# TensorE chooses among code versions by each expert's token count, in a kernel of local attention and a top-2 mixture of experts

## The chip, the cores and the metric

The kernel runs on one core of a Trainium2 chip. Besides TensorE (matmuls), VectorE (DVE), ScalarE (ACT) and GpSimd (POOL), SyncE (SP) issues DMAs, and 16 DMA engines move data between HBM and the on-chip memories. Each engine runs its own instruction stream, in order, and waits for others on semaphores. Matmul results go to PSUM, which has eight banks of 512 f32 columns by 128 partitions.

The metric is the device time of one execution in microseconds. Before the change three runs gave 741.88, 744.48 and 735.51 us, median 741.88.

## What is computed

Attention over four sequences of 768 tokens with eight heads (a local window of 16 and block summaries) gives 3072 tokens of 512 values. These go through a mixture of eight experts. Each token picks its two best experts by a noisy gate, and each expert applies two products with a ReLU between them:

```python
    N, D, E, F = (3072, 512, 8, 1024)
    ...
    logits = x @ w_gate
    noise_scale = np.log1p(np.exp(x @ w_noise))
    noisy_logits = logits + noise_scale * noise
    top2 = np.argpartition(-noisy_logits, 2, axis=1)[:, :2]
    ...
    for e in range(E):
        for k in range(2):
            mask = top2[:, k] == e
            if not mask.any():
                continue
            h = np.maximum(x[mask] @ w1[e], 0.0)
            out[mask] += top2_w[mask, k, None] * (h @ w2[e])
```

The mean count is 3072 x 2 / 8 = 768 tokens for an expert. With the reference's default inputs the counts are 728, 793, 748, 801, 765, 779, 756 and 774.

## The kernel before

The attention stage goes over 24 tiles of 128 tokens and takes the first 176 us or so. The gate runs beside it, in six batches; it gives each token a slot in each of its two experts' lists. An expert has `CAP = 816` slots. What does not fit goes to an overflow block at the end (L1023 to L1033), which is jumped over when `nover`, a count computed on VectorE in `count_over` (L552 to L564), is zero; all five engines load that count into a register (L1023) and branch on it (L1024). With the default inputs no expert overflows.

Then the experts follow one after another (L953 to L966). For expert e:

- `x_gather` (L625) fetches the tokens' rows from HBM by index, on GpSimd's queue, 128 slots at a time; `x_trans` (L636) transposes them into `xte` by a DMA on SP's queue.
- `mm1(e, half, f)` (L642 to L656) computes 128 of the 1024 hidden values, `f` from 0 to 7, for one half of the slots: columns 0 to 384 in half 0, 384 to 816 in half 1, so 384 or 432 columns. Weights and tokens are split into two f16 parts, so one `f` is 12 matmuls (three pairings of parts times four chunks of 128 input values), all on line 650, into one PSUM bank. ScalarE then writes the ReLU (`hth`, L654) and VectorE the remainder (`htl`, L655), over all columns of the half.
- `mm2(e, c, pv)` (L680 to L706) computes the second product for 128 slots, `c` from 0 to 5: 24 matmuls of 512 columns (L696). The last piece, `c == LAST == 6`, has only 48 slots. It is done as 48 matmuls of 256 columns (L692), two at a time in two halves of the output partitions. VectorE scales the result by the gate weight and adds the earlier sum (L703), and GpSimd scatters it to the output (L86).
- `prev_gather` fetches the earlier sums, and `next_loads` spreads the next expert's weight loads, splits and gathers over the steps of this one.

The first expert differs in order: its half 0 is computed while the last gate batches are still decoded, three pieces of its second product come ahead of its half 1 (L930 to L942).

The order of instructions on each engine is the order in which the code issues them, written out by hand. All choices are made at build time but the overflow block: every expert is computed for all 816 slots, whether a token stands in them or not; empty slots carry an index out of bounds, which the scatter drops.

PSUM is shared: two buffers `pt` for the second product, and a pool of four banks `h` for the first product and the last gate pieces (L872), opened when the attention's own buffers are given back (L871).

## Time and profile before

| what | value |
|---|---|
| median of 3 runs | 741.88 us |
| profiled execution | 741.86 us |
| its span, first to last instruction | 740.1 us |
| mean granted TensorE clock | 0.963 |
| attention and gate, about | 0 to 176 us |
| first two experts, with weight loads | 176 to 325 us |
| experts 2 to 7, each | 67.05 us |
| a hidden tile of half 0 / half 1 on TensorE | 1.95 / 2.19 us |
| the piece of 48 slots on TensorE | 2.74 us |

The page gives for each engine the busy time and its share of the span; then the span in 40 slices; the DMA queues; the chain of work that ended last, followed back from the last instruction to what released it at each step; and groups of instructions by line. "q8 instruction" is a DMA queue that brings code, not data. Names such as PEldq, DVEq or SPq mean an engine's sequencer: register loads, branches and semaphore instructions, which are not counted as busy time. PEld is the weight load that goes with each matmul and overlaps the matmul before it. A matmul's listed duration is longer than the distance from one start to the next, since matmuls are pipelined; the cost of one in a stream is that distance.

### The profile page before, as it was taken

To read this page: it belongs to the slowest core of one execution; us is meant where nothing else is said; L and a number is where in the kernel's file an instruction comes from. 1 tells how busy PE (TensorE), PEld (TensorE's weight loads), DVE (VectorE), ACT (ScalarE), POOL (GpSimd) and SP (SyncE) were. 2 spreads that over 40 slices of the span, in tenths; PEclk is the share of its full clock that TensorE was granted. 3 is DMA by queue.
4 is the path that set the end of the run, shared out by engine and by line. 5 is a ranking of instruction groups with operands and counts; after the bars stand their busy time and mean duration, and the time that the engine had idled before them with its cause. 6 is when DMAs were issued, how large, how long until landed. Compare 5 with 4: busy or idle time off the path is not lost.

```text
span 740.1 us, 13612 instructions
## 1 busy us (share of the span) xinstructions
PE 694.0 (94%) x5330; PEld 409.2 (55%) x5330; DVE 323.2 (44%) x686; ACT 234.8 (32%) x523; POOL 283.1 (38%) x464
## 2 busy tenths in 40 slices
PE   7979897887989999999999999999999999999992
PEld 6667686765535555455446545554654555455441
DVE  6647868685934344234414431541353143412210
ACT  3568766771404044024203310430242033102100
POOL 2566556443040550553234243414432342340141
PEclk9999988985999999999999999999999999999997
DMA  9998987273269698569826941993497289511020
GB/s 284 283 281 249 278 230 215 92 186 122 88 156 364 207 276 195 151 179 222 235 84 162 198 169 65 192 224 131 112 214 180 86 169 163 159 47 38 23 80 33
DMA packets 105418, 126.21 MB, mean 171 GB/s; under 512 B 63701, under 2 KB 68445, under 8 KB 105344
## 3 DMA queue, kind: packets, MB, share of 16 engines
q1 hardware_dynamic: 93200, 88.96, 48.0%
q0 software_dynamic: 12144, 36.28, 18.1%
q8 instruction: 44, 0.72, 0.5%
q14 instruction: 30, 0.25, 0.1%
HBM read 88.14 MB, written 26.36 MB: 155 GB/s over the span
## 4 chain that ended last, share of the span: by engine, by line
PE 73%; DMA 11%; DVE 9%; SPq 1%; ACT 1%; POOL 1%; issue 1%; POOLq 0%; DVEq 0%
PE h L650 32%; PE pt L696 29%; PE pt L692 3%; DMA vw<-in_vt_dram 2%; PE o L337 2%; DMA htl<-in_vb_dram 2%; PE s L304 2%; DMA stg<-in_vb_dram 2%; PE pt L324 1%; PE o L378 1%; DMA stg<-in_w_dram 1%; DMA xd<-xr 1%; DMA xg<-xd,tb 1%; DVE w1l L596 1%; DVE w2l L596 1%
## 5 line engine op out<-in xcount | busy, mean ns | idle before, releaser
L650 PE MATMUL h<-xte,w1h 128*128 128x432 f16 (+1 forms) x1024 | 201.9, 338 | 3.6 <-DVE htl L655 2.9
L654 ACT ACTIVATE hth<-h 128x432 f16<-128x432 f32 (+1 forms) x128 | 63.7, 507 | 287.9 <-PE h L650 284.7
L86 POOL DMA_INDIRECT out_dram<-y,tb x48 | 53.4, 1113 | 244.7 <-DVE y L703 214.0
L650 PEld LDWEIGHTS <-w1h 128*128 128x128 f16 x1024 | 99.9, 98 | 81.1 <-issue 7.2
L696 PEld LDWEIGHTS <-hth 128*128 128x128 f16 x768 | 75.1, 98 | 91.8 <-issue 2.3
L655 DVE SCALAR_TENSOR_TENSOR htl<-h,hth 128x432 f16<-128x432 f32 (+1 forms) x128 | 73.2, 580 | 96.2 <-ACT hth L654 94.5
L650 PE MATMUL h<-xte,w1l 128*128 128x432 f16 (+1 forms) x512 | 109.9, 338 | 0.0
L703 DVE SCALAR_TENSOR_TENSOR y<-pt,tb,prev 128x512 f32<-128x512 f32 x42 | 31.5, 750 | 149.2 <-PE pt L696 149.2
L86 POOL DMA_INDIRECT xg<-xd,tb x56 | 58.9, 1052 | 95.9 <-DMA xte<-xg 59.7
L696 PE MATMUL pt<-w2l,hth 128*128 128x512 f16 x384 | 91.0, 379 | 1.5 <-DVE w2l L596 1.5
L696 PE MATMUL pt<-w2h,htl 128*128 128x512 f16 x384 | 90.7, 379 | 0.0
L696 PE MATMUL pt<-w2h,hth 128*128 128x512 f16 x384 | 90.7, 379 | 0.0
L650 PEld LDWEIGHTS <-w1l 128*128 128x128 f16 x512 | 50.3, 98 | 38.8 <-issue 0.9
L587 ACT ACTIVATE w2h<-stg 128x1024 f16<-128x1024 f32 x32 | 33.8, 1055 | 92.4 <-DMA stg<-in_w_dram 92.4
L696 PEld LDWEIGHTS <-htl 128*128 128x128 f16 x384 | 37.6, 98 | 45.3
L596 DVE SCALAR_TENSOR_TENSOR w2l<-stg,w2h 128x1024 f16<-128x1024 f32 x32 | 39.1, 1222 | 52.5 <-ACT w2h L587 51.8
L86 POOL DMA_INDIRECT prev<-out_dram,tb x42 | 46.9, 1116 | 10.9 <-issue 10.9
L318 ACT ACTIVATE p<-s,nm 128x118 f32<-128x118 f32 x192 | 50.5, 375 | 0.8
L358 POOL TENSOR_TENSOR xr<-x,xr 128x512 f16<-128x512 f32 x24 | 30.3, 1261 | 50.6 <-ACT xr L355 43.3
L596 DVE SCALAR_TENSOR_TENSOR w1l<-stg,w1h 128x1024 f16<-128x1024 f32 x32 | 41.7, 1302 | 15.3 <-ACT w1h L587 12.3
L337 PE MATMUL o<-vw,pts 118*64 118x65 f32 x768 | 34.9, 247 | 5.7 <-DMA vw<-in_vt_dram 5.6
L337 PEld LDWEIGHTS o<-vw,pts 118*64 118x64 f32 x768 | 30.3, 158 | 11.8 <-DMA vw<-in_vt_dram 8.3
(164 smaller groups left out, 641.9 us busy)
## 6 DMA issues: line engine op xcount, KB each, us to landing
stg<-in_w_dram SPq DMA_DIRECT2D x64, 512.0 KB
vw<-in_vt_dram SPq DMA_DIRECT2D x48, 195.0 KB
q<-in_qt_dram SPq DMA_DIRECT2D x24, 256.0 KB
xd<-xr SPq DMA_DIRECT2D x24, 256.0 KB
kb<-in_kt_dram SPq DMA_DIRECT2D x6, 768.0 KB
out_dram<-prev SPq DMA_DIRECT2D x6, 768.0 KB
htl<-in_vb_dram SPq DMA_DIRECT2D x6, 390.0 KB
hth<-in_vb_dram SPq DMA_DIRECT2D x5, 390.0 KB
```

What stands on the lines that cost most here:

```text
L86: return nc.gpsimd.indirect_dma_start(**kw)
L318: nc.scalar.activation(PE_[t][:, a, hp, :], SC[t][:, a, hp, :], AF.Exp, bias=NM[t][:, 1, a, hp:hp + 1], scale=0.125)
L337: nc.tensor.matmul(o[64 * blk:64 * blk + 64, h // 4, c:c + D + 1], PT[t][:NK, h % 2, h // 2, 64 * blk:64 * blk + 64], VX[t][blk][:NK, h, : ...
L358: nc.gpsimd.tensor_tensor(XR[t][:, DM:], X[t], XR[t][:, 0:DM], op=OP.subtract)
L587: nc.scalar.activation(WT[e][n + "h"][:, i % 4, :], SG[e, i], AF.Copy, scale=sc)
L596: nc.vector.scalar_tensor_tensor(lo, SG[e, i], sc, hi, op0=OP.mult, op1=OP.subtract)
L650: nc.tensor.matmul(ph[:, :n], w[wn][:, c, f * P:(f + 1) * P], x[:, xo + c, c0:c1], start=(k == 0), stop=(k == 11))
L654: nc.scalar.activation(hh[:, f, c0:c1], ph[:, :n], AF.Relu)
L655: nc.vector.scalar_tensor_tensor(hl[:, f, c0:c1], ph[:, :n], 0.0, hh[:, f, c0:c1], op0=OP.max, op1=OP.subtract)
L692: nc.tensor.matmul(py[64 * i:64 * i + 64, :HD], hx[:, f, c * P:c * P + 64], wv[:, f, HD * i:HD * i + HD], start=(k == 0), stop=(k == 23), ...
L696: nc.tensor.matmul(py, hx[:, f, c * P:c * P + P], wv[:, f, :], start=(k == 0), stop=(k == 23))
L703: nc.vector.scalar_tensor_tensor(y, py[:, :d], gw, pv[:, :d], op0=OP.mult, op1=OP.add)
```

## The change

The first product's second half exists in four versions, ending at slot 744, 768, 792 or 816, with 360, 384, 408 or 432 columns. VectorE works out in `count_over`, by comparing each expert's count with 744, 768 and 792, which version an expert needs, and by comparing with 768 whether its last 48 slots are used at all; both numbers go to `arms`. TensorE loads the two into registers ahead of an expert's half 1 (`pick`). It then chooses by the first for each `f` of half 1, so eight times an expert, among four copies of the 12 matmuls, and by the second once an expert, whether the 48 matmuls of the last piece run. TensorE alone takes part in the choice; the other engines run the same instructions as before, over all 816 slots.

As the four banks and the two `pt` buffers are now written inside the versions, they are tiles set up once and taken in turn. VectorE clears columns 384 to 432 of the four banks once, since a narrow version leaves the last columns unwritten.

```diff
+    WIDTHS = range(744, CAP + 1, 24)
...
+        k = len(WIDTHS) - 1
+        ge = work.tile([P, E, k], F32, name="ge", bufs=1)
+        nc.vector.tensor_tensor(ge, cf[:, :, None].to_broadcast([P, E, k]),
+                                edges[:, None, :].to_broadcast([P, E, k]), op=OP.is_gt)
+        ga = work.tile([P, E, 2], F32, name="ga", bufs=1)
+        nc.vector.tensor_reduce(ga[:, :, 0], ge, axis=AX.X, op=OP.add)
+        nc.vector.tensor_scalar(ga[:, :, 1], cf, float(LAST * P), None, op0=OP.is_gt)
+        nc.vector.tensor_copy(arms, ga)
...
+    def pick(e):
+        _, v = nc.values_load_multi_w_load_instructions(
+            arms[0:1, e, :], engines=[mybir.EngineType.PE], min_val=0, max_val=len(WIDTHS) - 1,
+            skip_runtime_bounds_check_because="sums of comparisons, at most one for each edge")
+        ARM[e] = [{mybir.EngineType.PE: x} for x in v]
...
+    def mm1(e, half, f):
+        c0, c1 = (0, H0) if half == 0 else (H0, CAP)
+        ph = bank()[:, 0]
+        if half == 0:
+            mm1_mul(e, f, ph, c0, c1)
+        else:
+            for i in tc.Switch(ARM[e][0], len(WIDTHS)):
+                mm1_mul(e, f, ph, c0, WIDTHS[i])
+        mm1_out(f, ph, c0, c1)
...
-        py = psum.tile([P, 512], F32, name="pt", bufs=2)
+        py = back()
...
+        if last:
+            for i in tc.Switch(ARM[e][1], 2):
+                if i:
+                    mul()
+        else:
+            mul()
...
-    banks.append(ctx.enter_context(tc.tile_pool(name="banks", bufs=4, space=PSUM, reuse_waits="tile")))
+    bpool = ctx.enter_context(tc.tile_pool(name="banks", bufs=1, space=PSUM, reuse_waits="tile"))
+    for i in range(4):
+        x = bpool.tile([P, 1, 512], F32, name=f"h{i}")
+        nc.vector.memset(x[:, 0, H0:CAP - H0], 0.0)
+        banks.append(x)
...
+    pick(0)
     for f in range(FC):
         mm1(0, 1, f)
...
         for half in range(2):
+            if half:
+                pick(e)
             for f in range(FC):
                 mm1(e, half, f)
```

`mm1_mul` holds the 12 matmuls and `mm1_out` the ReLU and the remainder, as they stood in `mm1` before; `mul` holds the second product's matmuls. `bank` and `back` return the fixed tiles in turn.

## The prediction

> **What bounds the kernel now.** I read the page first (engine shares, clock, chain), then the chain of waits in order of time, then a table by stretch, then the single rows of TensorE.

> ```profile
> span 740.1 us, 13612 instructions
> PE 694.0 (94%) x5330; PEld 409.2 (55%) x5330; DVE 323.2 (44%) x686; ACT 234.8 (32%) x523; POOL 283.1 (38%) x464
> PE h L650 32%; PE pt L696 29%; PE pt L692 3%; DMA vw<-in_vt_dram 2%; PE o L337 2%; DMA htl<-in_vb_dram 2%; PE s L304 2%; DMA stg<-in_vb_dram 2%; PE pt L324 1%; PE o L378 1%; DMA stg<-in_w_dram 1%; DMA xd<-xr 1%; DMA xg<-xd,tb 1%; DVE w1l L596 1%; DVE w2l L596 1%
> ```

> Two thirds of the chain that ends last are the two expert products on TensorE. In order of time that chain is

> ```profile
> 178.13 3.87 PE h L650 x12
> 458.69 33.23 PE h L650 x192
> 491.91 31.08 PE pt L696 x144
> 522.99 2.74 PE pt L692 x48
> 724.19 2.76 PE pt L692 x48
> ```

> and by stretch (columns: length, busy time and count by engine, granted clock, DMA share, GB/s)

> ```profile
> 175.70:290.80 115.10, 109.01 (x623) 59.77 (x622) 57.49 (x141) 32.47 (x52) 31.14 (x55) 0.97 0.76 216
> 340.20:357.82 17.62, 17.62 (x98) 9.43 (x97) 9.07 (x12) 8.40 (x13) 7.49 (x12) 1.00 1.12 287
> 458.69:525.73 67.04, 67.04 (x385) 35.35 (x386) 23.30 (x31) 15.73 (x24) 24.54 (x42) 1.00 0.73 160
> ```

> An expert from the second on is 33.23 + 31.08 + 2.74 = 67.05 us of TensorE without a gap, at full clock; VectorE has 23.3 us of work in it, ScalarE 15.7, GpSimd 24.5, the DMA engines 0.73 of the time. So in this stage every microsecond put on or taken off TensorE moves the end by as much, and nothing else is near to becoming the bound.

> **What is taken away.** The second half of the first product is eight times 12 matmuls of 432 columns (L650), the first half of 384:

> ```profile
> 461.88 1.46 PE L650 MATMUL h<-xte,w1h 128*128 128x384 f16 x8
> 463.83 1.46 PE L650 MATMUL h<-xte,w1h 128*128 128x384 f16 x8
> 475.69 1.62 PE L650 MATMUL h<-xte,w1h 128*128 128x432 f16 x8
> 477.88 1.62 PE L650 MATMUL h<-xte,w1h 128*128 128x432 f16 x8
> ```

> From start to start 12 matmuls take 1.95 us at 384 and 2.19 us at 432 columns: 162.5 and 182.5 ns each, 0.417 ns a column. With the reference's default inputs I count 728, 793, 748, 801, 765, 779, 756 and 774 tokens for the eight experts. The versions end at 744, 768, 792 and 816 slots, so the experts save 72, 0, 48, 0, 48, 24, 48 and 24 columns, 264 in all: 264 x 96 matmuls x 0.417 ns = 10.6 us. The last 48 slots stay empty where the count is at most 768, in four experts: 4 x 2.74 = 11.0 us. Together 21.5 us, 2.9%, if choosing cost nothing.

> **What is added.** 64 choices among four versions (eight for each expert, one for each f) and 8 choices whether the last piece runs: 72 choices, so they may cost 21.5 / 72 = 0.30 us each before the gain is gone. Each choice is register arithmetic and a jump to the version on TensorE's own instruction stream, and a second jump from the version's end to the common code, past the versions that were not taken. The profile of before has one runtime condition, the overflow block at the end (L1023, L1024), which every engine jumps over:

> ```profile
> L1023 SPq FUSED_REGOPS  x1: 178/178/178, 632.2 to 632.2; - x1
> L1023 PEldq TENSOR_LOAD <-nover x1: 490/490/490, 725.6 to 725.6; - x1
> L1024 SPq EVENT_SEMAPHORE  x9: 2/17/17, 637.8 to 638.5; - x9
> L1024 POOLq EVENT_SEMAPHORE  x6: 17/30/43, 731.1 to 731.6; - x6
> L1024 ACTq EVENT_SEMAPHORE  x2: 17/17/17, 696.2 to 696.3; - x2
> L1024 PEldq EVENT_SEMAPHORE  x2: 51/51/51, 730.4 to 730.6; - x2
> L1024 DVEq EVENT_SEMAPHORE  x2: 21/21/21, 730.6 to 730.7; - x2
> L1024 SPq COMPARE_BRANCH  x1: 53/53/53, 632.6 to 632.6; - x1
> L1024 ACTq COMPARE_BRANCH  x1: 50/50/50, 693.7 to 693.7; - x1
> L1024 PEldq COMPARE_BRANCH  x1: 4162/4162/4162, 726.2 to 726.2; - x1
> L1024 DVEq COMPARE_BRANCH  x1: 72/72/72, 727.6 to 727.6; - x1
> L1024 POOLq COMPARE_BRANCH  x1: 62/62/62, 728.1 to 728.1; - x1
> ...
> q8 instruction: 44, 0.72, 0.5%
> ```

> The reader is to see that the branch itself lasts 50 to 72 ns on four engines, but the next instruction starts 5.2 us (SP), 2.5 (ACT), 2.9 (DVE) and 3.0 us (POOL) after it, and on TensorE the branch is recorded with the whole delay, 4.16 us. A jump over much code cost 2.5 to 5.2 us wherever it happened. The new jumps pass over less code (a version is 12 weight loads and 12 matmuls; the overflow block has 8 experts x 120 matmuls and as many weight loads), so whether they pay the same is the question on which all hangs. No row shows a short jump. I take 4.2 us, TensorE's own row; the ends are 0.05 us (the bare branches) and 5.2 us (SP's).

> [...]

> **How far TensorE's queue covers it.** The sequencer runs ahead of the array:

> ```profile
> L650 PEldq EVENT_SEMAPHORE  x22: 51/51/51, 177.9 to 672.6; - x22
> 659.89 33.23 PE h L650 x192
> ```

> The last wait that L650's sequencer handles, at 672.6, stands ahead of the second half, which starts on the array at 659.89 + 96 x 0.1625 = 675.5: a lead of 2.9 us, some 18 matmuls. Likewise the load of nover starts at 725.6 while the array works until 724.19 + 2.76 = 726.95. So a jump does not stop the array at once; the first 2.9 us of each half are covered. But a lead is refilled only if the sequencer needs less than the array for each f, and the array needs 1.8 to 2.2 us.

> **The sum.** One choice costs the sequencer S = 0.2 (register arithmetic, as SP's row) + 4.2 (jump in) + 4.2 (jump out) = 8.6 us; issuing the 12 pairs takes 12 x 2.74 / 48 = 0.7 us, which I let lie beside the fetch for the jump out. An f's matmuls run within that, even at half clock (the row 178.13: 12 matmuls in 3.87 us). So for an expert:
> - second half: two register loads 2 x 0.49 = 1.0, plus 8 x 8.6 = 68.8, less the lead 2.9, in place of 8 x 2.19 = 17.5: +49.4 us. The narrower matmuls then save nothing, since the array waits.
> - last piece: the lead in the second product is 18 x 31.08 / 144 = 3.9 us, against 4.4 for getting in: +0.5; then 4.2 out in place of 2.74, whether skipped or run: +1.5. Together +2.0.
> - the array works 2 of 8.6 us in that half and will drop to half clock for part of it, as in the row at 178.13; the second product then starts slow: estimate +2 (0 to 4).

> That is 53.4 us an expert, 8 x 53.4 = 427 us. In 175.70 to 290.80 the array idles 115.1 - 109.0 = 6.1 us on loads of the first two experts' weights; a later TensorE no longer waits there: -4.

> The small edits: four DVE instructions in count_over before the last copy,

> ```profile
> 199.73 0.33 DVE L559 TENSOR_TENSOR x<-cf,steps 128x168 f32<-128x168 f32 x1
> 200.65 0.17 DVE L564 CAST nover<-nf 128x9 int32<-128x9 f32 x1
> PE pt L696 <- DVE w2l L596: 1.5, 2, 1.0
> ```

> of 0.17 to 0.33 us, 0.8 us ahead of the split of w2 that TensorE waits for next: +0.8 (0 if the later work absorbs it). The four banks are now cleared by VectorE, once, 128x48 each, near 0.17 us by the small rows:

> ```profile
> 175.72 1.89 PE L378 MATMUL h<-wg,xt 128*128 128x16 f32 x8
> 177.04 0.32 DVE L522 TENSOR_TENSOR acc<-acc,o 128x168 f32<-128x168 f32 x1
> ```

> They stand behind L522 on VectorE, so the gate matmuls into the first bank can start at 177.36 + 0.34, not 175.72: +2.0, 0 if the waits after it absorb this. Fixed banks in turn, where the pool gave four before, and the two fixed tiles of the second product change no wait: the same four and two buffers with the same readers. One more iota on GpSimd lies at the start, where it has nothing due. No DMA is added or moved on SP's or GpSimd's queue; their gathers and scatters wait on TensorE's pace and stretch with it. ScalarE and VectorE still empty all 432 columns.

> Sum: 741.86 (profiled execution, span 740.1; the median of the runs is 741.88, the same) + 427 - 4 + 3 = 1168 us.

> **The rivals.**
> 1. The jump out costs little, because its target is asked for on entering the version or follows it at once. The bounds of S: jumps of 2.5 us (ACT's row) and a free way out give 0.2 + 2.5 + 0.7 = 3.4, +7.8 us for a half, about -1.4 for the last piece: 742 + 8 x 6.4 = 793; with 4.2 us in, S = 5.1 and about 742 + 8 x 22 = 918. For it: two jumps are not known to be equal. Against: 0.7 us of issue cannot cover a fetch of 4.2.
> 2. Faster, the other side: the versions lie so near that the jumps hit loaded code. Then S = 0.2 + 0.05 + 0.7 + 0.05 = 1.0 us, under the array's 1.8 to 2.2 us, the lead stays, and 742 - 21.5 + 3 = 723 us. This decides from S below about 1.9. For it: before, the instruction queue's 44 packets, 16 KB each, never show as idle time of TensorE, so straight code is fetched in time. Against: versions and jumps make the stream four times as long for the same work, and every jump row here is slow.
> 3. Jumps partly hit: S of 2.2 to 2.4, 0.2 us over the array for each f, about cancels the 11 us that the skipped pieces save, and the time is within 2%: some 740.
> That the kernel would not do what it says has no room of its own: were the counts higher, it would pay the same jumps.

> **How the numbers follow.** Forecast 0.76; rival 1 0.13; rival 2 0.07; rival 3 0.04. Slower by over 2% is forecast and rival 1: 0.89; within 2% (about what can be told from no change here): 0.04; faster: 0.07. Upper bound: SP's 5.2 us for both jumps and no overlap, S = 11.3, +71 for a half, +4 last piece, +4 clock: 742 + 8 x 79 = 1374. The likeliest one's own range is 918 (both jumps 2.5: S = 5.2, +22 an expert) to 1374. The range takes in the upper half of rival 1 and goes from 830 to 1400; left out are rivals 2 and 3 and the rest of rival 1.

> **What would show it.** Right: second halves of about 60 to 70 us for each expert with the 12 matmuls of an f together and gaps of some 6 us between, jumps of microseconds at the new lines of TensorE's sequencer, a granted clock of 0.5 there, more packets in the instruction queue than its 44 (one or two more for each choice), first halves unchanged at 15.6 us. Wrong in size: the first jump long and the second not. Wrong altogether: second halves of 15 to 17.5 us without gaps. Wrong in the cover: a gap already at the first f of the first half.

## The result, and the profile after

The changed kernel takes 1279.73 us (median of 4 runs, 1276.32 to 1281.57) against 743.18 us for the kernel before in the same series. The ratio is 1.7245, with a 95% interval of 1.711 to 1.7379. The profiled execution has a span of 1276.7 us, 536.6 more than before.

The page of the changed kernel, engine shares, granted clock by slice and the queue that brings code:

```profile
span 1276.7 us, 13978 instructions
PE 805.0 (63%) x5138; PEld 428.5 (34%) x5138; DVE 326.8 (26%) x694; ACT 234.5 (18%) x523; POOL 282.7 (22%) x465
...
PEclk9898969558866985689667966798569866797679
...
q8 instruction: 288, 4.72, 2.2%
```

TensorE runs 192 matmuls fewer and is busy 63% of a span that has grown by 73%; the other engines do the work they did before. From the eighth slice on, in which the choices begin, the clock drops to a half or two thirds again and again. The code queue has 288 packets instead of 44.

Who waited for whom on TensorE (total, times, longest):

```profile
PE h L675 <- issue: 386.2, 64, 15.9
PE h L675 <- DMA stg<-in_w_dram: 26.3, 4, 8.5
PE o L385 <- DVE lg L393: 8.4, 4, 4.0
```

L675 is the line of the first product's matmuls now. There are 64 waits, one for each choice of a version, 6.0 us in the mean, and they are put down to "issue": no other engine is late, TensorE's own instruction stream is. The sequencer's instructions around the choices, which the trace gives under L1126 (the line on which the program is closed), L685 and L740:

```profile
L1126 PEldq MOVE  x144: 29/29/34, 219.5 to 1258.1; - x144
L1126 PEldq COMPARE_BRANCH  x144: 299/4667/11380, 219.8 to 1264.0; - x144
L1126 ACTq COMPARE_BRANCH  x72: 32/33/33, 205.0 to 1229.9; - x72
L1126 DVEq COMPARE_BRANCH  x72: 41/41/53, 217.1 to 1256.9; - x72
L1126 PEldq FUSED_REGOPS  x72: 32/32/39, 219.7 to 1258.2; - x72
L1126 POOLq COMPARE_BRANCH  x72: 32/33/46, 222.2 to 1257.7; - x72
L1126 SPq COMPARE_BRANCH  x72: 20/33/113, 224.0 to 1032.3; - x72
...
L685 PEldq BRANCH_PREFETCH_HINT  x64: 31/40/50, 220.2 to 1225.9; - x64
...
L740 PEldq EVENT_SEMAPHORE  x4: 51/51/51, 315.4 to 1132.4; - x4
```

(The three numbers are the shortest, the middle and the longest duration in ns.) TensorE executes 144 branches, two for each of 72 choices. The middle one lasts 4.67 us, the longest 11.4. The register work beside them, moves and one fused operation, is some 30 ns each. TensorE is not alone in the choice, as I had described it: the four other engines pass each choice by a branch of their own, 20 to 113 ns.

What one choice looks like on the array, from the last expert's half, when the DMA engines are nearly idle:

```profile
1165.46 1.53 PE L675 MATMUL h<-xte,w1h 128*128 128x408 f16 x4 [7.59 <-issue]
1166.79 1.56 PE L675 MATMUL h<-xte,w1l 128*128 128x408 f16 x4
1168.15 1.56 PE L675 MATMUL h<-xte,w1h 128*128 128x408 f16 x4
1175.30 1.54 PE L675 MATMUL h<-xte,w1h 128*128 128x408 f16 x4 [5.59 <-issue]
```

The 12 matmuls of one f come together, at half clock (some 340 ns apart; at full clock 172 would do, between the 162.5 ns at 384 columns and the 182.5 at 432), and then the array is empty for 5.6 us. From one choice to the next it is 9.84 us. And by stretch, the same columns as before:

```profile
464.30:500.00 35.70, 8.17 (x25) 3.25 (x24) 4.13 (x5) 3.09 (x5) 5.74 (x10) 0.56 0.88 147
500.00:558.60 58.60, 21.85 (x72) 9.54 (x72) 7.17 (x9) 6.50 (x10) 0.00 (x0) 0.63 0.10 24
594.01:609.60 15.59, 15.59 (x86) 8.94 (x87) 5.62 (x8) 4.83 (x8) 8.90 (x17) 0.89 0.98 245
609.60:685.36 75.76, 36.04 (x109) 13.87 (x108) 11.40 (x14) 9.41 (x14) 2.10 (x4) 0.65 0.27 64
1136.26:1151.86 15.60, 15.60 (x86) 8.98 (x87) 3.35 (x6) 2.95 (x7) 3.33 (x6) 0.89 0.19 52
1151.86:1230.82 78.96, 31.38 (x108) 13.00 (x106) 5.69 (x10) 5.21 (x10) 0.00 (x0) 0.65 0.04 7
1230.82:1262.50 31.68, 31.25 (x144) 14.02 (x144) 4.43 (x7) 0.00 (x0) 10.05 (x18) 1.00 0.21 69
```

The first half of an expert still takes 15.6 us where the piece ahead of it was run. After a skipped piece it takes 17.3, as its first two f take 5.6 us instead of 3.9, at half clock for a part: the rows at 594.01 and 1136.26 have 86 of its 96 matmuls at a clock of 0.89, and its last 1.7 us lie in the rows behind them. The second half takes 94.3 us for one expert (the first two rows), 74.1 for the next and 77.3 for the last, where 17.5 stood before. The second product (the last row) is as before. In the first row the array got 25 matmuls in 35.7 us, while the DMA engines were busy 0.88 of the time.

### The profile page after: what moved, and what is told of

Its sections match the earlier page's. It is cut to its first block, busy times and chain, and to the rows that moved or that the text cites. A ratio compares the mean times of both kernels' runs of the same rounds, so it can differ in the third digit from the quotient of the medians.

```text
span 1276.7 us, 13978 instructions
## 1 busy us (share of the span) xinstructions
PE 805.0 (63%) x5138; PEld 428.5 (34%) x5138; DVE 326.8 (26%) x694; ACT 234.5 (18%) x523; POOL 282.7 (22%) x465
## 3 DMA queue, kind: packets, MB, share of 16 engines
q8 instruction: 288, 4.72, 2.2%
## 5 line engine op out<-in xcount | busy, mean ns | idle before, releaser
L675 PE MATMUL h<-xte,w1h 128*128 128x384 f16 (+3 forms) x1024 | 281.6, 420 | 421.4 <-issue 386.2
L675 PEld LDWEIGHTS <-w1h 128*128 128x128 f16 x1024 | 115.3, 119 | 561.2 <-issue 500.7
L86 POOL DMA_INDIRECT out_dram<-y,tb x48 | 57.0, 1187 | 793.2 <-DVE y L750 704.8
L692 ACT ACTIVATE hth<-h 128x432 f16<-128x432 f32 (+1 forms) x128 | 65.1, 509 | 889.3 <-PE h L675 856.3
L675 PE MATMUL h<-xte,w1l 128*128 128x384 f16 (+3 forms) x512 | 151.9, 436 | 0.0
L736 PE MATMUL pt<-w2h,hth 128*128 128x512 f16 x384 | 93.6, 388 | 6.2 <-ACT hth L692 6.2
L675 PEld LDWEIGHTS <-w1l 128*128 128x128 f16 x512 | 63.9, 125 | 64.2 <-issue 44.4
L86 POOL DMA_INDIRECT prev<-out_dram,tb x42 | 43.2, 1028 | 10.8 <-issue 10.8
L616 DVE SCALAR_TENSOR_TENSOR w1l<-stg,w1h 128x1024 f16<-128x1024 f32 x32 | 41.8, 1306 | 10.8 <-ACT w1h L607 9.7
L344 PE MATMUL o<-vw,pts 118*64 118x65 f32 x768 | 35.1, 249 | 5.4 <-DMA vw<-in_vt_dram 5.3
L344 PEld LDWEIGHTS o<-vw,pts 118*64 118x64 f32 x768 | 30.5, 160 | 11.3 <-DMA vw<-in_vt_dram 7.8
```

The lines of the kernel that those rows point to most:

```text
L86: return nc.gpsimd.indirect_dma_start(**kw)
L344: nc.tensor.matmul(o[64 * blk:64 * blk + 64, h // 4, c:c + D + 1], PT[t][:NK, h % 2, h // 2, 64 * blk:64 * blk + 64], VX[t][blk][:NK, h, : ...
L616: nc.vector.scalar_tensor_tensor(lo, SG[e, i], sc, hi, op0=OP.mult, op1=OP.subtract)
L675: nc.tensor.matmul(ph[:, :c1 - c0], w[wn][:, c, f * P:(f + 1) * P], x[:, xo + c, c0:c1], start=(k == 0), stop=(k == 11))
L692: nc.scalar.activation(hh[:, f, c0:c1], ph[:, :n], AF.Relu)
L736: nc.tensor.matmul(py, hx[:, f, c * P:c * P + P], wv[:, f, :], start=(k == 0), stop=(k == 23))
```

## The experiments

Ratios are against the kernel before, run in the same series.

**The same choices by conditions in line.** The same register, the same four versions, but no table:

```diff
-            for i in tc.Switch(ARM[e][0], len(WIDTHS)):
-                mm1_mul(e, f, ph, c0, WIDTHS[i])
+            v = ARM[e][0][mybir.EngineType.PE]
+            with tc.If(v < 2) as a:
+                with tc.If(v < 1) as b:
+                    mm1_mul(e, f, ph, c0, WIDTHS[0])
+                with b.Else():
+                    mm1_mul(e, f, ph, c0, WIDTHS[1])
+            with a.Else():
...
-            for i in tc.Switch(ARM[e][1], 2):
-                if i:
-                    mul()
+            with tc.If(ARM[e][1][mybir.EngineType.PE] > 0):
+                mul()
```

> The same choices with the same registers and the same versions, but made by nested two-way conditions whose code stands in line (a jump passes over 24 to 78 instructions) instead of a jump into a table; the last piece is one condition that jumps over 96 instructions. Code theory (the time goes into fetching code that a jump lands in, because each version of the table starts in code that is not loaded): short jumps land in loaded code, the sequencer stays ahead, both savings are kept but for what a jump now and then over the edge of the loaded code costs: 720 to 745 us, 728 the likeliest. Choice theory (any decision on TensorE's sequencer costs some 5 us, because the branch has to wait for the register or for the queue to run empty): 2 or 3 branches for each f, as slow as the table or slower: above 1200 us.

Measured: 749.66 us, ratio 1.014 (1.007 to 1.0211). The branches of this kernel on TensorE, by the line of the condition, and its code queue:

```profile
L686 PEldq COMPARE_BRANCH  x64: 73/147/3694, 220.5 to 695.0; - x64
...
L687 PEldq COMPARE_BRANCH  x64: 65/214/4764, 220.7 to 632.6; - x64
...
L692 PEldq COMPARE_BRANCH  x48: 70/176/298, 280.0 to 696.7; - x48
...
q8 instruction: 64, 1.05, 0.6%
```

More branches than in the table kernel, taken on the same values, and the middle one lasts 0.15 to 0.21 us instead of 4.67. The choice theory falls: neither reading the register nor deciding is slow. Of the 537 us all but 9 are gone, though the same versions stand in the program; their code came in 64 packets instead of 288.

The times of the code packets in both traces show what a long branch waits for. Here TensorE's branches at the choices are sorted by the packets of the code queue that start and land while the branch lasts:

| kernel | packets inside | branches | shortest / middle / longest, us |
|---|---|---|---|
| changed kernel | 0 | 9 | 0.30 / 0.34 / 1.98 |
| changed kernel | 1 | 39 | 2.85 / 3.72 / 9.57 |
| changed kernel | 2 | 96 | 4.37 / 4.75 / 11.38 |
| conditions in line | 0 | 179 | 0.07 / 0.18 / 1.74 |
| conditions in line | 1 | 9 | 2.78 / 3.69 / 4.76 |

A branch with packets inside ends 1.3 to 2.2 us after the last of them has landed. So in these two traces a long branch is a wait for code.

The expected 728 us was missed, too, and its range of 720 to 745 us: 13 of the branches, about one for five f, last 0.4 to 4.8 us (the others 65 to 336 ns), and the matmuls wait for issue and for `htl`, where the kernel before has 0.2 and 2.9 us:

```profile
PE h L675 <- DVE htl L702: 11.5, 4, 7.2
...
PE h L675 <- issue: 5.4, 5, 1.8
...
PE pt L745 <- issue: 3.7, 3, 1.8
```

**The small edits alone.** Counts and fixed banks; no choice is made. The register loads still stand in the source, but this kernel does not run them: line 664, theirs, has only semaphore instructions in its trace.

```diff
-            for i in tc.Switch(ARM[e][0], len(WIDTHS)):
-                mm1_mul(e, f, ph, c0, WIDTHS[i])
+            mm1_mul(e, f, ph, c0, c1)
...
-            for i in tc.Switch(ARM[e][1], 2):
-                if i:
-                    mul()
+            mul()
```

> The small edits alone: counts on VectorE, register loads on TensorE, fixed banks cleared by VectorE; every expert runs all 816 slots and no choice is made. My prediction priced these at +3 us: 743 to 748. If the register loads or the fixed banks carry a part of the loss, more than 760.

Measured: 744.37 us, ratio 1.004 (1.0009 to 1.007): 3.6 us over the 740.81 beside it. The line of the register loads, and two waits that the change brings:

```profile
L664 PEldq EVENT_SEMAPHORE  x8: 51/51/51, 221.4 to 674.4; - x8
```

```profile
PE h L675 <- DVE cf L568: 2.0, 1, 2.0
PE h L385 <- DVE h L919: 1.9, 1, 1.9
```

The matmuls wait 1.9 us for the clearing of the bank, which I had priced at 2.0. L568 is the line in `count_over` that reads the counts out of a bank; that bank is taken again sooner in the new order of turns, which I had said would change no wait. What the register loads cost, this run does not show; the kernel with the conditions in line runs all eight and loses 9 us altogether, so they are not the loss either.

**The choice of the last piece alone, by the table** (the second half runs 432 columns).

> The eight choices for the last piece alone, by the table; the second half of the first product always runs 432 columns. From the gaps in the trace after the change (4.3 us between the products around a skipped piece, where 2.74 would run; 1.7 us more around a piece that runs): 8 x 1.6 = +13 on top of the small edits: 752 to 762 us. My prediction had +2.0 an expert, 16 us. If a jump out of an empty version were covered by the queue: 4 x 2.7 saved, about 735.

Measured: 759.23 us, ratio 1.0256 (1.0208 to 1.0304), 14.9 over the kernel without choices. So of the 537 us some 15 belong to the last piece and the register loads, which this kernel runs, and 520 to the 64 choices among versions. Why skipping costs more than running shows in the changed kernel's branches where it skips the piece of the seventh expert:

```profile
L1126 PEldq COMPARE_BRANCH  x2: 342/1939/3536, 1128.6 to 1132.6; - x2
...
L740 PEldq EVENT_SEMAPHORE  x4: 51/51/51, 315.4 to 1132.4; - x4
```

The jump in lasts 0.34 us only. Then the empty version has one instruction, a semaphore wait at 1132.4, 3.5 us later: TensorE waits until its own queued matmuls are done. The instruction waits for the semaphore that the last matmul before it raises as it ends (1132.4), and raises it in place of the matmuls that are left out. Only then the jump out begins, 3.5 us with the queue empty. The array is empty from 1132.4 to 1136.3: 3.9 us, more than the 2.74 us of work that it leaves out.

**All four versions 432 columns wide.**

```diff
-                mm1_mul(e, f, ph, c0, WIDTHS[i])
+                mm1_mul(e, f, ph, c0, c1)
```

> All four versions run 432 columns, so the choice is between equal versions and nothing is saved by narrower matmuls. Code theory: the sequencer sets the pace in those halves, the array waits either way: 1270 to 1290 us, no change from the changed kernel. Width theory (the narrower matmuls still bring their 10.6 us): 1285 to 1300.

Measured: 1265.83 us (2 runs). Not slower than the changed kernel: the narrower matmuls bring nothing there. It came out 1% faster, below the range; its 128 jumps at the choices of a version add up to 625 us against 634 in the changed kernel, and from 2 runs I make nothing of the rest.

**Two versions instead of four.**

```diff
-    WIDTHS = range(744, CAP + 1, 24)
+    WIDTHS = range(768, CAP + 1, 48)
```

> The same table with two versions, 384 and 432 columns, instead of four, so a version is always next to the code ahead of the table or next to the code behind it. In the trace of the change the jumps next door cost 1.2 to 1.3 us less than the others (in: 3.5 for the first version, 4.7 for the rest; out: 3.4 for the last, 4.8 for the rest). Five of the eight experts took a middle version. Code theory: 5 x 8 x 1.25 = 50 us less than the changed kernel, some 1230 us (1210 to 1245). If the price of a choice has nothing to do with where its code lies: no change, 1280 us.

Measured: 1207.05 us (2 runs), 73 us less than the changed kernel; expected were 35 to 70. The direction is the code theory's. In the single branch records of the later f (the fourth to the eighth) the first version is entered in 2.9 us and left in 4.9, the last one entered in 4.7 and left in 3.3; the middle versions of the changed kernel cost 4.7 in and 4.8 out. So a neighbour is 1.4 to 1.8 us cheaper, not 1.25, on 40 choices. The code packets say why: in both kernels, in these f, each jump into the first version and each out of the last has one packet inside, all others two.

**One choice an expert.** All eight f of the second half in one version, with eight PSUM banks; the last piece as in the change.

```diff
+    def mm1_some(e, fs, spaces):
+        for i in tc.Switch(ARM[e][0], len(WIDTHS)):
+            for f, ph in zip(fs, spaces):
+                mm1_mul(e, f, ph, H0, WIDTHS[i])
```

> One choice an expert instead of eight: all eight f of the second half stand in one version, with eight banks of PSUM. The table choice of the last piece stays. Per-choice price: the eight dear choices of an expert become one, whose way out is asked for some 15 us ahead of use, and whose way in is covered by the queue's lead of 2.9 us less 1.0 us for the register loads: 3 to 8 us an expert are left, less the 1.3 us of narrower matmuls: 757 + 8 x (2 to 7) = 770 to 810 us. If the loss lay in anything that goes with the number of versions or matmuls and not with the number of choices, it would stay above 1000.

Measured: 801.41 us (2 runs), ratio 1.0809 (1.0734 to 1.0884), inside the range. Eight choices in place of 64, with as many matmuls and versions, take 478 us off. The time went with the number of jumps.

**The same, announced.** The registers are read and the jump's target is announced ahead of the first half:

```diff
-            if half:
+            if not half:
                 pick(e)
+                tc.switch_hint(ARM[e][0], len(WIDTHS), label=f"v{e}")
```

> As the kernel with one choice an expert, but the choice is read and the jump's target announced to the code fetch ahead of the first half, 16 us before the jump. If announcing makes the fetch run beside the matmuls: the way in costs some 0.3 us and lies within the lead, 759 - 10.6 = about 748 us (744 to 755). If announcing does nothing: as without it, but for the 1.0 us of loads that move out of the lead: 762 to 802.

Measured: 765.75 us, ratio 1.0316 (1.0263 to 1.0369). The jump lines of the two kernels, the announced one second:

```profile
L1144 PEldq COMPARE_BRANCH  x32: 308/1784/10402, 226.7 to 784.0; - x32
```

```profile
L1146 PEldq COMPARE_BRANCH  x32: 298/334/4266, 227.2 to 751.2; - x32
```

In the single records the way into the second half falls from 3.3 to 10.4 us to 0.3 us for six of the seven later experts (1.9 for the other). So announcing works, and what the jump had waited for can be fetched beside matmuls. It also settles that the jump through a table is not slow in itself: the same branch lasts 0.3 us when its target has been announced. The expected 748 was missed by 18 us, because I had not looked at what else stands there. The first expert's second product waited for the clearing of the added banks; and a skipped piece left a gap (5.1 us ahead of the fourth expert), after which the next expert started at half clock for a part. In this kernel's waits and one stretch (the stretch is the first product of the fourth expert, behind a skip; from its first matmul to the first of its second product it takes 35.1 us, in the kernel without choices 33.1):

```profile
PE h L675 <- issue: 25.5, 7, 5.5
PE pt L741 <- DVE pt L988: 7.2, 1, 7.2
...
407.61:442.56 34.95, 34.95 (x192) 19.35 (x192) 15.79 (x22) 14.14 (x22) 11.11 (x18) 0.94 1.06 237
```

**The choice of the last piece alone, in line.** The second condition of the first experiment alone.

> The choice of the last piece alone, by a condition in line that jumps over 96 instructions. In the trace of the kernel with conditions in line a skipped piece left a gap of 0.5 us where 2.74 would run, and a piece that runs cost nothing: 744.4 - 4 x 2.2 = 735.6 us (733 to 739). Choice theory: as the table, 757 to 762.

Measured: 741.75 us, ratio 1.0008 (0.9983 to 1.0033). Expected were 735.6, 733 to 739. A skipped piece leaves a gap of 0.3 us and saves 2.4, as expected, in experts three, five and seven: from the second product of the second expert to the end of the last this kernel takes 429.1 us, the one without choices 436.3. But the first expert's saving is lost, and the second expert ends 4.0 us later. In this kernel's waits:

```profile
PE h L675 <- DVE htl L692: 4.5, 3, 4.0
...
PE h L675 <- issue: 2.2, 1, 2.2
```

The 2.2 us stand ahead of the first expert's second half, where a register load lasts 2.57 us; the 4.0 us in the second expert's first product, where `htl` stands in VectorE's queue among the splits of weights, and those wait 11.4 us there for the weights of the second product (9.0 without choices).

**Code fetched while no data moves.** The changed kernel, with the next expert's loads, splits and gathers moved out of the second half:

```diff
                 mm1(e, half, f)
-                ticks(e)
+                if half == 0:
+                    ticks(e)
...
             mm2(e, c, pv[c])
             ticks(e)
+            while tick[0] < min(23, 11 + 3 * c):
+                ticks(e)
```

> The changed kernel with the next expert's weight loads, splits and gathers taken out of the second half (they are issued in the first half and during the second product), so that code is fetched while the DMA engines are nearly idle. In the changed kernel's trace the first two choices of a half take 6.7 + 8.1 and 6.5 + 4.3 us, the later ones 4.7 + 4.4, and a packet of code starts up to 7 us after the jump that asks for it while data moves. Load theory (code waits behind data on the DMA queues): the first two choices fall to the others' 9 us or so: 7 experts x 7 us less, about 1230 us (1215 to 1250), unless loads come late for the next expert. Place theory (the first jumps after a long stretch without any are dear whatever the DMA does): they stay at 14.8 and 10.8 us, 1265 to 1290.

Measured: 1262.53 us (2 runs). The total misses its range. The sums of the two jumps of a choice, mean over the second to the seventh expert, for f = 0 to 7, from the single branch records:

| | 0 | 1 | 2 | 3 | 4 | 5 | 6 | 7 |
|---|---|---|---|---|---|---|---|---|
| changed kernel | 15.9 | 11.0 | 8.8 | 9.3 | 9.0 | 8.9 | 9.0 | 8.9 |
| loads moved | 11.7 | 9.2 | 8.6 | 8.7 | 8.8 | 8.9 | 8.8 | 8.8 |

The first two choices lose 6.0 us together and the others nothing to speak of, as the load theory had it (7 us): all 64 choices fall from 634 to 586 us. The gain is given back in the second product, into which the moved work now crowds:

```profile
PE pt L736 <- DVE y L750: 25.6, 12, 3.7
```

TensorE waits there for VectorE's results, since the splits stand ahead of them in VectorE's queue. The f = 0 choice keeps 2.9 us over the rest; part of the loads still run then, and what the rest of it is stays open.

**What the choices can bring.** One choice an expert, read and announced after the second f of the first half, the last piece in line, the added banks cleared early and narrowly.

> One choice an expert, read and announced during the first half, and the last piece by a condition in line; the clearing of the four added banks stands ahead of the gate's last pieces and covers 72 columns instead of 432. From the kernel with the announced choice, 765.8: around a skipped piece its trace has gaps of 5.5 us and a half-speed start of 2 us after them, where the condition in line left 0.5 (4 x 7 = 28), around a piece that runs 1.1 and 2 us, where it left nothing (4 x 3 = 12), and the second product of the first expert started 5.7 us later behind the clearing: 766 - 28 - 12 - 5 = 721 by that sum; the first two experts are paced by weight loads and will take some of it: 728 us (720 to 735), faster than both. If jumps in line and announced jumps still cost a lead that is not refilled: 741 or more.

Measured: 739.34 us (12 runs), ratio 0.9945 (0.9916 to 0.9974) against 743.61: faster than both kernels, but by half a per cent, not by two, and outside the 720 to 735 us. The stretches of the second expert's first product and of experts three to eight, and a wait:

```profile
255.00:300.00 45.00, 37.04 (x198) 20.03 (x196) 18.72 (x26) 13.97 (x23) 19.57 (x34) 0.89 0.91 242
333.74:727.50 393.76, 388.65 (x2161) 204.76 (x2160) 131.04 (x179) 85.80 (x136) 140.50 (x240) 1.00 0.60 145
...
PE h L675 <- DVE htl L698: 8.1, 2, 7.8
```

Six experts take 393.8 us where 6 x 67.05 = 402.3 stood. Of the 14.9 us that these six should save (192 columns x 96 x 0.417 ns = 7.7, and three pieces at 2.4) 8.5 are left; two of the announced jumps still took 3.0 and 4.7 us. The second expert loses 8 us on `htl`, whose writer stands behind a split of weights that come late, and the clock falls to 0.89 there.

**The first expert without a choice.** The last kernel, but the first expert runs all 816 slots; the banks that only its choice needed early are cleared later or not at all.

> As the kernel with one announced choice an expert and the condition in line, but the first expert runs all 816 slots without a choice, as before the change. In the traces its saving was lost: the second expert's first half waits for weight loads (a gap of 7.8 us there, after which TensorE runs at half speed for a while, against 1.5 us in the kernel without choices), so the whole second expert ended 7 us later than without choices although it began earlier. From the third expert on the kernel with the announced choice was 8 us faster than the one without. Load-bound start: the second expert ends where it does without choices, the rest keeps its 8 us and the second expert's own piece adds little: 744.4 - 8 to 12 = 732 to 736 us, 1.0 to 1.6% below the kernel before. If the first experts' loss has another cause (the banks, the code fetch): no change from 739.

Measured: 741.20 us (12 runs), ratio 0.9963 (0.9932 to 0.9995), not the 732 to 736 expected. The wait of 7.8 us is gone, but in this kernel's profile the second expert's announced jump took 7.05 us:

```profile
PE pt L675 <- issue: 5.7, 1, 5.7
```

So announcing does not always help. In the three kernels with it, experts two to eight make 21 announced jumps. Of these 16 last 0.3 to 0.4 us, and in each case a packet of code starts between the announcement and the jump. In the four that last 3.0 to 7.0 us none does, and in the fifth, of 1.9 us, it starts 0.6 us ahead of the jump. Busy DMA engines do not explain it: in the last two kernels their share in between was 0.69 to 0.85 for seven jumps that were short, and 0.69, 0.80, 0.81 and 0.94 for the four long ones. Why some announcements bring no packet, and whether these first experts could keep their saving, is open.

## Why the prediction was right, and where it was off

- **The bound.** TensorE without gaps, nothing else near: shown. Where choices were taken away the time came back to 744. Of the 537 us lost, 386 are TensorE's waits for issue in the first product and 111 are more busy time (805.0 against 694.0, at a mean clock of 0.78 against 0.963).
- **The jumps are dear, and hide the saving.** Right. The same decision by a short jump costs 0.15 to 0.21 us and by the table 4.7, and with versions of equal width the kernel is no slower. I had left open whether a short jump pays the price; the runs showed that what counts is not how many instructions a jump passes over in the source but whether the code at its end is loaded: with no packet of code inside, a jump lasts 0.3 us in the middle, with one or two 3.7 and 4.8. The short jump that an announced target makes says the same. The packets are 244 more for 72 choices, at 16.4 KB each (4.72 MB by 288), over three for a choice where I had looked for one or two; how the table is laid out in memory, no run here shows.
- **Its price.** This term was too small. I had S = 8.6 us a choice; with the DMA idle it is 9.84, because a jump is 4.7 and not 4.2 us and the instructions around it take 0.5 and not 0.2. The 4.2 us came from a jump with one packet of code inside (TensorE's jump over the overflow block, 726.19 to 730.35 us in the trace of before; the packet takes 727.88 to 728.82); most of the new ones have two. Both numbers are read by one load for an expert, 0.56 us in the middle, not by two of 0.49. For the last expert's second half that makes 77.3 us where the prediction has 66.9.
- **The same price for every f.** This was wrong. While the next expert's data moves, the first two choices cost 15.9 and 11.0 us in jumps instead of 9. Moving the loads took most of that away. The mean second half of experts three to eight is 84.2 us, worked out from the starts of their matmuls: 17.3 over the prediction, of which 10.4 stand in the quiet half too and some 6.9 are load; with the loads moved this mean falls to 77.8. From start to start these six experts take 816.7 us where 402.4 stood, 69.0 more for each instead of 53.4. That is 94 of the 1279.7 - 1168 = 112 us of the miss. The range, 830 to 1400 us, is wide enough to hold it; that is due to the spread of the jumps' rows, 2.5 to 5.2 us, and not to a good estimate.
- **The way out.** I let the issue of the version lie beside the fetch and took 4.2 us for the jump out. Rival 1 had it nearly free. Every version does begin with an announcement of its way out (the 64 hints of L685), but the branch follows some 0.2 us later, as the matmuls are handed to the queue at once; so 4.7 us remain, and rival 1 falls. With 14 to 17 us between announcement and jump, as in the kernel with one choice an expert, it worked: 0.3 to 0.9 us.
- **The lead.** The queue's 2.9 us are not refilled, as predicted: each of the 64 choices left the array waiting, 6.0 us in the mean.
- **The last piece, +2.0 an expert.** The size was near: 1.2, as from the start of the last full matmul to the next expert's first it takes 4.24 us in the mean of experts three to seven in place of 3.05; in the run with this choice alone 14.9 / 8 = 1.9, register loads included. The mechanism for a skip was not: the jump into an empty version took 0.30 to 0.34 us, and a wait for TensorE's own queue, which I had not thought of, comes ahead of the jump out (3.5 us in the seventh expert).
- **The slow start of the second product, +2.** It did not come there: 31.25 us busy at clock 1.00 in the row at 1230.82. The clock is back as soon as the second product begins; the drop lies inside the second half (0.56 to 0.65 in its rows), where it costs nothing as the sequencer is later. A slow start came elsewhere: behind a skipped piece, with the array empty for 3.9 us, the next expert's first half takes 1.7 us more.
- **The first two experts, -4.** Wrong sign: from the first expert's start to the third's it went from 146.5 to 267.1 us, 60 an expert, more than the 53.4 without any credit. That is the other 18 us of the miss.
- **Rival 2**, jumps that hit loaded code, is what the conditions in line do: 179 of their 188 branches have no packet of code inside. Its 723 us were not reached there. A jump that waits for code in about every fifth f, and `htl` behind the weights' splits in the start, are the two waits that grew; how the 27 us divide, no run shows.

## What to carry to other kernels

Price a runtime choice by the code that its jumps have to wait for, not by the number of its branches (here 4.7 us for a jump into the table, 0.15 to 0.21 us for a branch in line): look for the one jump that the profile already has, and set it against the engine's queue lead and the work between two choices. If a choice is worth making, make it once for much work (8 choices in place of 64 took 478 us off), announce it early (0.3 to 0.4 us for 16 of 21 announced jumps), or let it jump only a short way in line; and look what an empty version must wait for (3.5 us here, ahead of its jump out). A saving in a stage that is bound by loads can be lost until the loads move: with the last piece chosen in line the second expert ended 4.0 us later than without choices.
